# Strided attention of five batches on GpSimd and VectorE instead of TensorE, and TensorE's insertions regrouped

## The chip, the cores and the metric

The kernel runs on one core of a Trainium2 chip. TensorE multiplies matrices, VectorE and ScalarE work element by element from SBUF and PSUM, GpSimd from SBUF alone, and SyncE issues the transfers. The time is that of the device for one execution, in microseconds (us); the runs are summed up by their median.

## The reference, cut to what matters

Attention with 8 batches, 8 heads, 576 positions and 64 columns per head, then a mixer. Heads 0 to 3 see the last 32 positions, heads 4 to 7 see earlier positions with the same remainder by 32:

```python
rel = pos[:, None] - pos[None, :]
mask_local = (rel >= 0) & (rel < stride)
mask_strided = (rel >= 0) & (pos[None, :] % stride == pos[:, None] % stride)
attn = np.exp(scores - max); attn = attn / (sum + 1e-09); out = np.matmul(attn, v)
# x: the heads side by side, 8 x 576 x 512
h = np.maximum(xt @ w_tok1, 0.0) @ w_tok2      # xt: x transposed, 512 x 576; w_tok1 576 x 256
u = x + h.transpose(0, 2, 1)
out = u + np.maximum(u @ w_ch1, 0.0) @ w_ch2   # w_ch1 512 x 1536
```

A strided head is thus 32 separate causal attentions over 18 positions.

## The kernel before, in words

All matmuls of the mixer keep f32 precision by splitting each operand into a high and a low part (`xh` and `xlo`, `hh` and `hl`, `uh` and `ul`, `gh` and `gl`), and take three products. The 4608 tokens go through the channel mixer (`mlp`) in nine groups of 512. A group has 12 hidden tiles `fc`. `up_proj(fc)` is 12 matmuls into a PSUM tile `h` (two banks); ScalarE makes `gh` of it (L454), VectorE the residual `gl` (L455); `down_proj(fc)` is 12 matmuls into four accumulators `acc`, issued after `up_proj(fc + 2)`. At the end VectorE (L483) and GpSimd (L485) make `ot`, in two buffers, and SyncE stores it.

A group has 48 slots, four per tile, at which other work is put into TensorE's queue; that queue's order is as written. In group g the other work is for batch b = g + 1:

- attention in units. A strided unit (`strided_unit`) is two heads and half of the positions, four per batch; it packs three of the 18-position attentions into one 64 x 64 product (12 small matmuls for the scores, 3 transposes, 12 matmuls for the values). A local unit is two heads and 384 positions (24 + 3 + 24). Score tables are masked and their maximum taken by VectorE (L144), exponentiated by ScalarE (L147), the output scaled by VectorE (L191, L252). A strided unit loads `eq`, `ek`, `ev`, a local one `lq`, `lk`, `lv`; both store to DRAM (`xs`, `xl`). Group 0 has four units, group 1 eight, groups 2 to 5 seven, group 6 six.
- at slot 33 or later `do_load` brings `x` of the batch back from DRAM with rows of one position in one partition; five slots later `tok1` multiplies it by `w_tok1` in five chunks, for each of which ScalarE makes `xh` (L292) and VectorE `xlo` (L293), two buffers each; then `tok2` transposes `x` into the same PSUM tile as the second product and makes `uh`, `ul` for the next group (its rest at slots 2 and 4 of that group).

A unit is a generator that is sent PSUM tiles in three steps. Before, one insertion holds the values of unit k - 2, the transposes of unit k - 1 and the scores of unit k, and shares one pair of banks:

```python
pair = [ps_t.tile() for _ in range(2)]
if av: av.send([t[:, :DT] for t in pair])
if tr: tr.send(ps_h.tile("h"))
if qk: qk.send([t[:, DT:] for t in pair])
```

The order on the other engines, SyncE's transfers included, is made by a scheduler from priorities and modelled times when the kernel is built; at run time each engine takes its queue in that fixed order and waits where an operand is missing.

Of the kernel before, what the change touches and what calls it, by code (L numbers as in the profile page):

```python
# [19 lines left out]
HL = 4  # L20
# [46 lines left out]
@with_exitstack  # L67
def attn_mixer_kernel(ctx, tc, qT, kT, vw, qsT, ksT, vsP, mask, w1, w2, wt1, wt2, outT):
    nc = tc.nc
# [437 lines left out]

    pools = {n: ctx.enter_context(tc.tile_pool(name=n, bufs=2, reuse_waits="tile")) for n in ("sp", "wk")}
    NS = 4 * NFC
    local_order = [(p, hp, c0) for p in range(1, B // 2) for c0 in (0, 3, 6) for hp in range(2)]  # L510

    for g in range(NG):
# [15 lines left out]

# [4 lines left out]
        if b < B:  # L533
            units = [lambda hp=hp, half=half: strided_unit(pools["sp"], pools["wk"], ps_t, b, hp, half) for hp in range(2) for half in range(2)]
            if g:
                n = 4 if g == 1 else 3
                for _ in range(n):
                    if local_order:
                        p, hp, c0 = local_order.pop(0)
                        units.append(lambda p=p, hp=hp, c0=c0: local_unit(pools["late"], pools["wk"], ps_t, p, hp, c0, 3))  # L540
                order = [u for pair in zip(units[:4], units[4:]) for u in pair] + units[4 + min(4, len(units) - 4):]
                order += [u for u in units if u not in order]
                units = order
# [5 lines left out]
            live = [None] * len(units) + [None] * 2  # L549

            def load(k, u, live=live):
                live[k] = u()
                next(live[k])

            def go(k, live=live):
                insert(live[k - 2] if k > 1 else None, live[k - 1] if 0 < k <= len(live) - 2 else None, live[k] if k < len(live) - 2 else None)

            for k, u in enumerate(units):
                at(max(0, first + tick * k - 6), lambda k=k, u=u: load(k, u))
            for k in range(len(units) + 2):  # L560
                at(first + tick * k, lambda k=k: go(k))
            last = first + tick * (len(units) + 1)
# [14 lines left out]
def _layout(q, k, v, moe_w_tok1, moe_w_tok2, moe_w_ch1, moe_w_ch2):  # L577
# [42 lines left out]
    for m in range(3):  # L620
        for a in range(4):
# [23 lines left out]
```

## Time and profile before

| | |
|---|---|
| median of 3 runs | 930.91 us (928.67 to 931.06) |
| the profiled execution | 929.39 us |
| its span (first to last instruction) | 927.6 us |
| TensorE / VectorE / ScalarE / GpSimd busy | 875.5 / 329.0 / 309.6 / 82.4 us |
| a group with seven units (group 5) | 97 us |
| a group without units (group 7) | 75 us |

All durations below come from the profiled execution. A group is counted from the end of the one before; its first microseconds hold the rest of the last one's output. "Busy" on TensorE is modelled per matmul; the distance between starts tells the pace.

### The profile page before, as it was taken

How to read it: one execution, taken by the hardware profiler on the slowest of the kernel's cores; microseconds unless marked ns; L12 is line 12 of the kernel's file. 1: busy time of each engine (PE TensorE's matmuls, PEld its weight loads, DVE VectorE, ACT ScalarE, POOL GpSimd, SP SyncE). 2: the span in 40 equal slices, each digit the busy share in tenths (PEclk: the TensorE clock that was granted, in tenths of full speed). 3: DMA queues.
4: the chain of work that ended last, by engine and by line, in shares of the span. 5: the costliest groups of instructions: out<-in, count | busy, mean ns of one | idle time of the engine just before them, and what ended most of it. 6: DMA issues, size and time to landing. Idle time of an engine off the chain costs nothing.

```text
span 927.6 us, 18575 instructions
## 1 busy us (share of the span) xinstructions
PE 875.5 (94%) x7412; PEld 694.8 (75%) x7412; DVE 329.0 (35%) x1215; ACT 309.6 (33%) x1085; POOL 82.4 (9%) x68
## 2 busy tenths in 40 slices
PE   5677899999989999999999999999999999999996
PEld 3455677787768877887778777877788787788885
DVE  4977772333323232323223333333233323111212
ACT  6755352225422343225322542145214421110110
POOL 1324330010001000020002000200020002001100
PEclk9998799999999999999999999999999999999999
DMA  8665752113440144014411351124311211000001
GB/s 276 200 206 165 222 169 64 42 46 100 119 134 23 56 117 143 16 61 122 128 44 46 109 157 43 46 71 142 97 46 33 74 42 46 1 1 24 23 1 46
DMA packets 65431, 81.21 MB, mean 88 GB/s; under 512 B 6976, under 2 KB 53440, under 8 KB 65344
## 3 DMA queue, kind: packets, MB, share of 16 engines
q1 hardware_dynamic: 65344, 80.01, 28.8%
q8 instruction: 59, 0.97, 0.4%
q14 instruction: 28, 0.23, 0.1%
HBM read 61.57 MB, written 18.28 MB: 86 GB/s over the span
## 4 chain that ended last, share of the span: by engine, by line
PE 83%; DMA 6%; DVE 5%; ACT 2%; SPq 2%; issue 1%; DVEq 0%; POOL 0%; ACTq 0%; POOLq 0%
PE acc L465 31%; PE h L451 30%; PE t L61 20%; PE h L64 2%; DMA w_raw<-in_w 1%; DVE w_f L103 1%; DVE w_f L104 1%; DMA xs<-ax 1%; DMA out_t<-ot 1%; DVE xlo L293 1%; SPq L275 1%; ACT as L147 1%; ACT xh L292 1%; DMA ev<-in_vsP 1%; DMA w_raw<-in_wt 1%
## 5 line engine op out<-in xcount | busy, mean ns | idle before, releaser
L451 PE MATMUL h<-uh,w1h 128*128 128x512 f32 x432 | 173.5, 402 | 5.1 <-DVE gl L455 5.1
L465 PE MATMUL acc<-gh,w2h 128*128 128x512 f32 x432 | 172.9, 400 | 0.0
L451 PE MATMUL h<-ul,w1h 128*128 128x512 f32 x432 | 170.5, 395 | 0.0
L451 PE MATMUL h<-uh,w1l 128*128 128x512 f32 x432 | 169.6, 393 | 0.0
L465 PE MATMUL acc<-gl,w2h 128*128 128x512 f32 x432 | 169.0, 391 | 0.0
L465 PE MATMUL acc<-gh,w2l 128*128 128x512 f32 x432 | 168.6, 390 | 0.0
L455 DVE SCALAR_TENSOR_TENSOR gl<-h,gh 128x512 fp32r<-128x512 f32 x108 | 74.5, 690 | 234.4 <-ACT gh L454 234.2
L454 ACT ACTIVATE gh<-h 128x512 fp32r<-128x512 f32 x108 | 64.1, 594 | 253.2 <-PE h L451 253.0
L147 ACT ACTIVATE as<-as,am 128x64 f32<-128x64 f32 x336 | 112.5, 336 | 44.8 <-DVE am L144 44.8
L485 POOL TENSOR_TENSOR ot<-ot,ul 128x512 f32<-128x512 f32 x32 | 40.6, 1290 | 687.5 <-DVE ot L483 687.5
L451 PEld LDWEIGHTS h<-uh,w1h 128*128 128x128 f32 x432 | 81.9, 190 | 23.5 <-DVE gl L455 5.6
L451 PEld LDWEIGHTS h<-uh,w1l 128*128 128x128 f32 x432 | 82.0, 190 | 17.3
L465 PEld LDWEIGHTS acc<-gh,w2l 128*128 128x128 f32 x432 | 81.3, 188 | 17.7
L465 PEld LDWEIGHTS acc<-gh,w2h 128*128 128x128 f32 x432 | 81.3, 188 | 17.7
L451 PEld LDWEIGHTS h<-ul,w1h 128*128 128x128 f32 x432 | 82.0, 190 | 16.1 <-DVE ul L349 0.3
L465 PEld LDWEIGHTS acc<-gl,w2h 128*128 128x128 f32 x432 | 81.3, 188 | 15.4
L144 DVE CUSTOM_DVE_ANT_0 as<-t,mask_sb 128x64 f32<-128x64 f32 x336 | 53.0, 220 | 36.0 <-PE t L61 29.5
L349 DVE TENSOR_TENSOR ul<-t,uh 128x512 fp32r<-128x512 f32 (+7 forms) x64 | 29.2, 457 | 100.0 <-ACT uh L348 99.9
L147 ACT ACTIVATION_READ_ACCUMULATOR as<-as,am 128x1 f32 x336 | 63.0, 187 | 0.0
L348 ACT CAST uh<-t 128x512 fp32r<-128x512 f32 (+7 forms) x64 | 25.3, 399 | 109.4 <-PE t L61 109.0
L293 DVE TENSOR_TENSOR xlo<-x,xh 128x512 fp32r<-128x512 f32 (+1 forms) x45 | 29.7, 678 | 56.0 <-ACT xh L292 56.0
L292 ACT CAST xh<-x 128x512 fp32r<-128x512 f32 (+1 forms) x45 | 24.8, 571 | 59.2 <-PE t L61 24.9
(62 smaller groups left out, 938.3 us busy)
## 6 DMA issues: line engine op xcount, KB each, us to landing
w_raw<-in_w SPq DMA_DIRECT2D x24, 512.0 KB
out_t<-ot SPq DMA_DIRECT2D x36, 256.0 KB
lv<-in_vw SPq DMA_DIRECT2D x20, 384.0 KB
ev<-in_vsP SPq DMA_DIRECT2D x32, 192.0 KB
eq<-in_qsT SPq DMA_DIRECT2D x32, 167.0 KB
ek<-in_ksT SPq DMA_DIRECT2D x32, 167.0 KB
lk<-in_kT SPq DMA_DIRECT2D x20, 208.0 KB
x<-xs SPq DMA_DIRECT2D x32, 128.0 KB
```

The lines of the kernel that those rows point to most:

```text
L61: self.tc.stamp_issue_order_token(self.tc.nc.tensor.matmul(*args, **how).ins, self.pool.name)
L144: nc.vector.tensor_tensor_reduce(out=s_t[:, c, j, :], in0=sc[j][:, 64 * c:64 * c + 64], in1=mask_sb[:, m, :], scale=-SCALE, scalar=TOP, op ...
L147: nc.scalar.activation(out=s_t[:, c, j, :], in_=s_t[:, c, j, :], func=AF.Exp, bias=m_t[:, c, j:j + 1], scale=-1.0, accum_out=z_t[:, c, j:j ...
L292: nc.scalar.copy(out=xh, in_=x)
L293: nc.vector.tensor_tensor(out=xlo, in0=x, in1=xh.bitcast(F32), op=ALU.subtract)
L348: nc.scalar.copy(out=uh, in_=pu)
L349: nc.vector.tensor_tensor(out=ul, in0=pu, in1=uh.bitcast(F32), op=ALU.subtract)
L451: nc.tensor.matmul(ph, l[:, cc, fs], r, start=(cc == 0 and k == 0), stop=(cc == NCC - 1 and k == 2))
L454: nc.scalar.activation(out=gh, in_=ph, func=AF.Relu)
L455: nc.vector.scalar_tensor_tensor(out=gl, in0=ph, scalar=0.0, in1=gh.bitcast(F32), op0=ALU.max, op1=ALU.subtract)
L465: nc.tensor.matmul(acc[cc], l[:, fc, cs], r, start=(fc == 0 and k == 0), stop=(fc == NFC - 1 and k == 2))
L485: add.tensor_tensor(out=o_t, in0=o_t, in1=ul.bitcast(F32), op=ALU.add)
```

## The change

Batches 0 to 2 (`NPE = 3`) keep their strided units. For batches 3 to 7 a new function `strided(pool, b)` puts one attention of 18 positions of one head into each of the 128 partitions (4 heads x 32). For query i GpSimd multiplies its 64 columns with those of each key up to i, at most nine keys an instruction, and VectorE sums over the columns; then softmax over a table of 18 x 18; then for each i GpSimd multiplies weights and values and VectorE sums over the keys. That is 27 products and 27 sums in either half, with two buffers `sprod` between the engines. The result goes to DRAM in the order of positions, so `load_x` fetches it in three transfers instead of eight. It is issued in group g for batch g + 2, with a priority behind everything else, into pool `sp` with one buffer, which opens late in group 1 where the strided units' pool `third` closes.

The insertions change too: the scores of unit k stand with the transposes of unit k - 1, and the values of a unit stand apart, each with a pair of banks of its own. Groups 2 to 6 keep only local units, one each six slots.

```diff
+def strided(pool, b):
+        q_t = pool.tile([P, NJ, D], F32, name="sa")
+        k_t = pool.tile([P, NJ, D], F32, name="sb")
+        nc.sync.dma_start(out=q_t, in_=qs[b - NPE])
+        nc.sync.dma_start(out=k_t, in_=ks[b - NPE])
...
+        for i in range(NJ):
+            for n0 in range(0, i + 1, NJ // 2):
+                n = min(i + 1 - n0, NJ // 2)
+                pr = pool.tile([P, NJ * D // 2], F32, name="sprod", bufs=2)[:, :n * D].rearrange("p (n d) -> p n d", d=D)
+                nc.gpsimd.tensor_tensor(out=pr, in0=k_t[:, n0:n0 + n], in1=q_t[:, i:i + 1].to_broadcast([P, n, D]), op=ALU.mult)
+                nc.vector.tensor_reduce(out=s_t[:, i, n0:n0 + n], in_=pr, axis=AX.X, op=ALU.add)
+        v_t = pool.tile([P, D, NJ], F32, name="sa")
+        nc.sync.dma_start(out=v_t, in_=vs[b - NPE])
...
+        o_t = pool.tile([P, NJ, D], F32, name="sb")
+        for i in range(NJ):
+            n = i + 1
+            nd = D if n <= NJ // 2 else D // 2
+            for d0 in range(0, D, nd):
+                pr = ...
+                nc.gpsimd.tensor_tensor(
+                    out=pr, in0=v_t[:, d0:d0 + nd, :n], in1=s_t[:, i:i + 1, :n].to_broadcast([P, nd, n]), op=ALU.mult)
+                nc.vector.tensor_reduce(out=o_t[:, i, d0:d0 + nd], in_=pr, axis=AX.X, op=ALU.add)
+        for h in range(HL):
+            nc.sync.dma_start(out=xd[1][b][:, D * h:D * h + D].rearrange("(j r) c -> r j c", r=ST), in_=o_t[ST * h:ST * h + ST])
...
-        def insert(av, tr, qk):
-            pair = [ps_t.tile() for _ in range(2)]
...
+        def scores(u, before):
+            if u:
+                u.send([ps_t.tile() for _ in range(2)])
+            if before:
+                before.send(ps_h.tile("h"))
...
-            first, tick = (6, 3) if g else (10, 5)
+            first, tick, half_tick, ahead = ((10, 5, 3, 6), (6, 3, 2, 4))[g] if g < 2 else (6, 6, 3, 4)
...
+                at(t, lambda k=k: qk(k))
+                at(t + tick + half_tick, lambda k=k: av(k))
...
+            if g == 1:
+                at(last + 1, third_ends)
+            if g and g + 2 < B:
+                at(i0, lambda: do_strided(g + 2))
```

How the instructions move on the engines is seen at four places. The lines are those of either kernel: after the change the numbers are higher (L293 `xlo` is L331, L455 `gl` is L493, L483 `ot` is L521).

TensorE, group 5, one insertion between large matmuls (`ev`, `ek`, `eq` of strided units, `as` the score table, `ident` the transposes), before:

```order
L451 MATMUL h<-uh,w1l 128x512
L61 MATMUL t<-ev,as 64x64 x12
L64 MATMUL h<-ident,as 128x128 x3
L61 MATMUL t<-ek,eq 64x64 x12
L451 MATMUL h<-uh,w1h 128x512
```

and after the change, group 3, where only local units (`lk`, `lq`) are left:

```order
L503 MATMUL acc_4476<-gh,w2l 128x512
L62 MATMUL t<-lk,lq 32x64 x24
L65 MATMUL h<-ident,as 128x128 x3
L503 MATMUL acc_4477<-gh,w2h 128x512
```

The values no longer stand there, and there are fewer such places.

VectorE, the token mixing of a middle group and what follows it, before (group 5):

```order
L455 SCALAR_TENSOR_TENSOR gl<-h,gh 128x512
L252 TENSOR_TENSOR ax<-t,az 128x3x64 x2
L455 SCALAR_TENSOR_TENSOR gl<-h,gh 128x512
L293 TENSOR_TENSOR xlo<-x,xh 128x512 x2
L455 SCALAR_TENSOR_TENSOR gl<-h,gh 128x512
L293 TENSOR_TENSOR xlo<-x,xh 128x512 x3
L305 SCALAR_TENSOR_TENSOR hl_7289<-t,hh_7288 128x512
L305 SCALAR_TENSOR_TENSOR hl_7291<-t,hh_7290 128x512
L349 TENSOR_TENSOR ul<-t,uh 128x128 x4
L483 TENSOR_TENSOR ot<-acc_6396,uh 128x512
L483 TENSOR_TENSOR ot<-acc_6397,uh 128x512
```

and after the change (group 3; `ss<-sprod` is a sum of products, `sm` the maximum of the strided softmax):

```order
L283 TENSOR_REDUCE ss<-sprod 128x7
L283 TENSOR_REDUCE ss<-sprod 128x9
L331 TENSOR_TENSOR xlo<-x,xh 128x512
L283 TENSOR_REDUCE ss<-sprod 128x8
L331 TENSOR_TENSOR xlo<-x,xh 128x512
L283 TENSOR_REDUCE ss<-sprod 128x9
L331 TENSOR_TENSOR xlo<-x,xh 128x512
L283 TENSOR_REDUCE ss<-sprod 128x9
L286 TENSOR_REDUCE sm<-ss 128x18
L287 TENSOR_TENSOR ss<-ss,sm 128x324
L343 SCALAR_TENSOR_TENSOR hl_5307<-t,hh_5306 128x512
L343 SCALAR_TENSOR_TENSOR hl_5309<-t,hh_5308 128x512
```

Between the `xlo` of chunks 2, 3 and 4 there stands a sum, which waits for a product of GpSimd.

VectorE a little later, at the border to group 4, after the change (`sb<-sprod` are sums of the value half):

```order
L387 TENSOR_TENSOR ul<-t,uh 128x256
L521 TENSOR_TENSOR ot<-acc_4475,uh 128x512
L521 TENSOR_TENSOR ot<-acc_4476,uh 128x512
L301 TENSOR_REDUCE sb<-sprod 128x64 x2
L493 SCALAR_TENSOR_TENSOR gl<-h,gh 128x512
L521 TENSOR_TENSOR ot<-acc_4477,uh 128x512
L301 TENSOR_REDUCE sb<-sprod 128x32 x2
L521 TENSOR_TENSOR ot<-acc_4478,uh 128x512
L493 SCALAR_TENSOR_TENSOR gl<-h,gh 128x512
```

Before, only `ot` stood ahead of the first `gl` there; now sums stand among them.

SyncE in the next group, after the change (`xs_87<-sb` is the strided result of batch 5, `x<-xs_87` its way back):

```order
L524 DMA out_t<-ot 128x512 x4
L158 DMA lq<-in_qT 128x384
L159 DMA lk<-in_kT 128x416
L272 DMA sa<-in_qs 128x1152
L303 DMA xs_87<-sb 32x18x64 x4
L158 DMA lq<-in_qT 128x384
L159 DMA lk<-in_kT 128x416
L317 DMA x<-xs_87 128x4x256
L319 DMA x<-xs_87 64x256 x2
L273 DMA sb<-in_ks 128x1152
L160 DMA lv<-in_vw 128x768
```

The store, which waits for the last sum of batch 5, stands ahead of a local unit's `lq` and `lk`; the load of the next batch's keys (`sb<-in_ks`) stands behind them.

## Rows read from the trace of the kernel before

**Rows 1.** The page: busy time of each engine with its share of the span and its instructions; then the chain of work that ended last, as shares by engine.

```profile
PE 875.5 (94%) x7412; PEld 694.8 (75%) x7412; DVE 329.0 (35%) x1215; ACT 309.6 (33%) x1085; POOL 82.4 (9%) x68
...
PE 83%; DMA 6%; DVE 5%; ACT 2%; SPq 2%; issue 1%; DVEq 0%; POOL 0%; ACTq 0%; POOLq 0%
```

**Rows 2.** The table of stretches, group 5 (with batch 6) and group 7 (no attention work beside it). Columns: the stretch in us, its length, busy us and instructions of TensorE, of its weight loads, of VectorE, ScalarE and GpSimd, TensorE's granted clock as a share of 2.4 GHz, the share of the DMA engines, GB/s.

```profile
590.00:687.00 97.00, 96.39 (x886) 76.93 (x885) 30.81 (x137) 33.21 (x125) 5.08 (x4) 1.00 0.29 84
...
783.00:858.00 75.00, 75.00 (x336) 61.06 (x335) 13.10 (x20) 9.52 (x16) 5.08 (x4) 1.00 0.04 15
```

**Rows 3.** VectorE's timeline, the residual `gl` of a hidden tile: of group 5 tile 3, tile 7 and tile 10, of group 6 tile 3, tile 4 and tile 10, of group 7 tile 3 and tile 10. Columns: start and length in us, engine, line, operation, out<-in, shapes, count, and in brackets the idle time before and what ended it.

```profile
606.65 0.69 DVE L455 SCALAR_TENSOR_TENSOR gl<-h,gh 128x512 fp32r<-128x512 f32 x1 [0.94 <-ACT gh L454]
...
636.69 0.69 DVE L455 SCALAR_TENSOR_TENSOR gl<-h,gh 128x512 fp32r<-128x512 f32 x1 [2.11 <-ACT gh L454]
...
659.79 0.69 DVE L455 SCALAR_TENSOR_TENSOR gl<-h,gh 128x512 fp32r<-128x512 f32 x1 [4.30 <-ACT gh L454]
...
704.54 0.69 DVE L455 SCALAR_TENSOR_TENSOR gl<-h,gh 128x512 fp32r<-128x512 f32 x1 [0.82 <-ACT gh L454]
...
710.66 0.69 DVE L455 SCALAR_TENSOR_TENSOR gl<-h,gh 128x512 fp32r<-128x512 f32 x1 [2.09 <-ACT gh L454]
...
755.42 0.69 DVE L455 SCALAR_TENSOR_TENSOR gl<-h,gh 128x512 fp32r<-128x512 f32 x1
...
802.51 0.69 DVE L455 SCALAR_TENSOR_TENSOR gl<-h,gh 128x512 fp32r<-128x512 f32 x1 [0.67 <-ACT gh L454]
...
840.53 0.69 DVE L455 SCALAR_TENSOR_TENSOR gl<-h,gh 128x512 fp32r<-128x512 f32 x1 [4.75 <-ACT gh L454]
```

**Rows 4.** TensorE's timeline around one insertion in group 5 (large matmul before, values of a local unit's neighbour, transposes, scores, large matmuls after), and the first scores of a later insertion. The profile counts each small f32 matmul twice.

```profile
629.52 0.39 PE L465 MATMUL acc<-gh,w2l 128*128 128x512 f32 x1
629.84 0.58 PE L61 MATMUL t<-ev,as 64*64 64x64 f32 x24
630.35 0.55 PE L64 MATMUL h<-ident,as 128*128 128x128 f32 x3
630.88 0.84 PE L61 MATMUL t<-ek,eq 64*64 64x64 f32 x24
631.65 0.50 PE L465 MATMUL acc<-gh,w2h 128*128 128x512 f32 x1
631.98 0.39 PE L465 MATMUL acc<-gl,w2h 128*128 128x512 f32 x1
...
637.71 0.52 PE L61 MATMUL t<-lk,lq 64*32 64x64 f32 x6 [0.54 <-DVE ax L191]
```

**Rows 5.** GpSimd: all instructions of the output's second addition (name, count, shortest/median/longest in ns, first and last start, shapes), the one instruction on 256 columns, and, from its timeline, the longest one.

```profile
L485 POOL TENSOR_TENSOR ot<-ot,ul x32: 1278/1290/1297, 183.9 to 859.8; 128x512 f32<-128x512 f32 x32
...
L126 POOL TENSOR_TENSOR t1l<-w_f,t1h x1: 727/727/727, 25.5 to 25.5; 64x256 fp32r<-64x256 f32 x1
...
111.44 1.74 POOL L116 TENSOR_TENSOR w1l<-w_f,w1h 128x512 fp32r<-128x512 f32 x1 [1.30 <-ACT w1h L115]
```

**Rows 6.** VectorE: the subtraction `xlo` in all its uses (shortest/median/longest in ns), the scaling of a strided unit's output (busy us, mean ns | idle us), and from the timeline two score tables that follow each other directly.

```profile
L293 DVE TENSOR_TENSOR xlo<-x,xh x45: 408/692/1501, 26.6 to 766.5; 128x512 fp32r<-128x512 f32 x35, 128x256 fp32r<-128x256 f32 x10
...
L252 DVE TENSOR_TENSOR ax<-t,az 128x192 f32<-128x192 f32 x64 | 19.9, 352 | 35.1 <-PE t L61 35.1
...
607.85 0.22 DVE L144 CUSTOM_DVE_ANT_0 as<-t,mask_sb 128x64 f32<-128x64 f32 x1 [0.51 <-PE t L61]
...
608.00 0.22 DVE L144 CUSTOM_DVE_ANT_0 as<-t,mask_sb 128x64 f32<-128x64 f32 x1
```

**Rows 7.** The timeline of ScalarE, VectorE and TensorE's weight loads in group 4's token mixing of batch 5: chunk 2's `xh` and `xlo` and the weight load that takes it; chunk 4's `xlo` and the weight load that takes it.

```profile
569.79 0.62 ACT L292 CAST xh<-x 128x512 fp32r<-128x512 f32 x1 [2.12 <-PE t L61]
570.45 0.69 DVE L293 TENSOR_TENSOR xlo<-x,xh 128x512 fp32r<-128x512 f32 x1 [2.05 <-ACT xh L292]
...
571.20 0.19 PEld L61 LDWEIGHTS t<-xlo,t1h 128*128 128x128 f32 x1 [0.28 <-DVE xlo L293]
...
573.31 0.69 DVE L293 TENSOR_TENSOR xlo<-x,xh 128x512 fp32r<-128x512 f32 x1 [0.81 <-ACT xh L292]
...
574.05 0.18 PEld L61 LDWEIGHTS t<-xlo,t1h 64*128 64x128 f32 x1 [0.50 <-DVE xlo L293]
```

**Rows 8.** The timeline near 30 us, in the part before the groups: two GpSimd subtractions that follow each other, a VectorE `xlo` on 256 columns beside them, and the matmul that waits for it.

```profile
30.22 3.07 POOL L116 TENSOR_TENSOR t2l<-w_f,t2h 128x512 fp32r<-128x512 f32 x2 [3.98 <-ACT t2h L115]
...
30.67 1.49 DVE L293 TENSOR_TENSOR xlo<-x,xh 128x256 fp32r<-128x256 f32 x1
...
32.21 0.58 PE L61 MATMUL t<-xlo,t1h 128*128 128x256 f32 x1 [1.07 <-DVE xlo L293]
```

**Rows 9.** The timeline at the border between groups 4 and 5: the third `ot` of group 4, `gl` of group 5's tile 0, and the first matmul of the third `up_proj`.

```profile
589.52 0.69 DVE L483 TENSOR_TENSOR ot<-acc,uh 128x512 f32<-128x512 f32 x1 [2.94 <-DMA out_t<-ot]
...
590.13 0.68 DVE L455 SCALAR_TENSOR_TENSOR gl<-h,gh 128x512 fp32r<-128x512 f32 x1
...
591.58 0.39 PE L451 MATMUL h<-uh,w1h 128*128 128x512 f32 x1
```

**Rows 10.** The chain of work that ended last: a load of `lq`, a store of attention output to DRAM, and SyncE issuing a transfer (start and length in us).

```profile
30.18 3.25 DMA lq<-in_qT
...
260.72 2.46 DMA xs<-ax
...
263.33 0.31 SPq L275
```

More of the change, by code (lines that the diff above doesn't have):

```diff
@@ L35 @@
 FIRST = {0: 1, 4: 2}
+NPE = 3
 NCC = DM // P
@@ L153, in local_unit @@
     def local_unit(pool, work, ps_t, p, hp, c0, n, into=None):
-        q_t = pool.tile([P, UC * P], F32, name="lq")[:, :n * P]
-        k_t = pool.tile([P, UC * P + 32], F32, name="lk")[:, :n * P + 32]
+        q_t = pool.tile([P, UC * P], F32, name="lq", bufs=1 if p else 2)[:, :n * P]
+        k_t = pool.tile([P, UC * P + 32], F32, name="lk", bufs=1 if p else 2)[:, :n * P + 32]
         v_t = pool.tile([P, 4 * UC, D], F32, name="lv")[:, :4 * n]
@@ L270, in load_x @@
         src = xd[half][b]
-        if half:
+        if half and b < NPE:
             src = src.rearrange("(r j) d -> r j d", j=NJ)
@@ L506, in staging_ends, with third_ends, do_strided @@
         pools["late"] = ctx.enter_context(tc.tile_pool(name="late", bufs=2, side="right", reuse_waits="tile"))
-    pools = {n: ctx.enter_context(tc.tile_pool(name=n, bufs=2, reuse_waits="tile")) for n in ("sp", "wk")}
+    pools = {"wk": ctx.enter_context(tc.tile_pool(name="wk", bufs=2, reuse_waits="tile"))}
+    third = tc.tile_pool(name="third", bufs=2, reuse_waits="tile")
+    pools["third"] = third.__enter__()
+    def third_ends():
+        third.__exit__(None, None, None)
+        pools["sp"] = ctx.enter_context(tc.tile_pool(name="sp", bufs=1, reuse_waits="tile"))
+    def do_strided(b):
+        now = tc.cur_priority
+        tc.cur_priority = now + 3000
+        strided(pools["sp"], b)
+        tc.cur_priority = now
     NS = 4 * NFC
@@ L533, in attn_mixer_kernel @@
         if b < B:
-            units = [lambda hp=hp, half=half: strided_unit(pools["sp"], pools["wk"], ps_t, b, hp, half) for hp in range(2) for half in range(2)]
+            st, loc = [], []
+            if b < NPE:
+                st = [lambda hp=hp, half=half: strided_unit(pools["third"], pools["wk"], ps_t, b, hp, half) for hp in range(2) for half in range(2)]
             if g:
[L536 to L543, printed above, removed]
+                for p, hp, c0 in local_order[:4 if g == 1 else 3]:
+                    loc.append(lambda p=p, hp=hp, c0=c0: local_unit(pools["late"], pools["wk"], ps_t, p, hp, c0, 3))
+                del local_order[:len(loc)]
+            units = [u for k in range(4) for us_ in (st, loc) for u in us_[k:k + 1]]
             if g == 0:
@@ L547, in attn_mixer_kernel @@
                 at(NS - 1, staging_ends)
-            first, tick = (6, 3) if g else (10, 5)
-            live = [None] * len(units) + [None] * 2
+            first, tick, half_tick, ahead = ((10, 5, 3, 6), (6, 3, 2, 4))[g] if g < 2 else (6, 6, 3, 4)
+            live = [None] * len(units)
             def load(k, u, live=live):
@@ L553, in load, with qk, av @@
                 next(live[k])
-            def go(k, live=live):
-                insert(live[k - 2] if k > 1 else None, live[k - 1] if 0 < k <= len(live) - 2 else None, live[k] if k < len(live) - 2 else None)
+            def qk(k, live=live):
+                scores(live[k] if k < len(live) else None, live[k - 1] if k else None)
+            def av(k, live=live):
+                live[k].send([ps_t.tile() for _ in range(2)])
             for k, u in enumerate(units):
[L559 to L562, printed above, removed]
+                t = first + tick * k
+                at(max(0, t - ahead), lambda k=k, u=u: load(k, u))
+                at(t, lambda k=k: qk(k))
+                at(t + tick + half_tick, lambda k=k: av(k))
+            at(first + tick * len(units), lambda: qk(len(live)))
+            last = first + tick * len(units) + half_tick
             i0 = max(last + 2, 33)
@@ L608, in grp_t @@
         return np.concatenate([a, np.zeros((B, HL // 2, P, TW * NT + TC - TW - S), a.dtype)], axis=3)
+    qs, ks = (c(grp(a)[NPE:]).reshape(B - NPE, P, NJ, D) for a in (q, k))
+    vs = c(grp(v)[NPE:].transpose(0, 1, 2, 4, 3)).reshape(B - NPE, P, D, NJ)
     vsP = np.zeros((B, HL, NT * TW, D), v.dtype)
```

22 lines of the change are left out of this document (14 added, 8 removed).

## The prediction

> **What bounds the kernel now.** I read the page first: TensorE is busy 94% of the span and makes 83% of the chain that ended last [rows 1]. A busy TensorE is no proof of a full one, so the second view is the table of stretches: from 590 to 687 us (group 5 with batch 6 beside it) TensorE shows 96.4 of 97 us at a granted clock of 1.00 (2.4 GHz), VectorE 31, GpSimd 5 [rows 2]. The third is the cadence inside it. The residual `gl` comes once per hidden tile, and where nothing is inserted (group 7) seven tiles take 840.53 - 802.51 = 38.0 us, 168 large matmuls at 0.226 us each. In group 5 the same seven take 659.79 - 606.65 = 53.1 us, with four strided and three local units between, and in group 6 755.42 - 704.54 = 50.9 us, with four and two [rows 3]. The reader is to see that in groups 2 to 6 the attention's small matmuls sit on the path one for one: what leaves TensorE's queue shortens the group, and what TensorE waits for lengthens it.
>
> **TensorE's gain.** A local unit costs 53.14 - 50.88 = 2.3 us (rounded) in such a stretch, so four strided units cost 53.1 - 38.0 - 3 x 2.3 = 8.3 us. One insertion seen singly agrees: from the last matmul before it (629.52) to the second after it (631.98) stand 2.46 us, of which two cadences are 0.45, so 2.0 us for a unit's values, transposes and scores [rows 4]. Its edges cost 0.1 us each: 629.52 to 629.84 and 631.65 to 631.98 instead of 0.23. The change splits what stood in one place into two, so in groups 2 to 5 three units now need seven places (four more than the three that the 2.3 us cover), 4 x 0.2 = 0.8 us. Gain 8.3 - 0.8 = 7.5 us, and 7.7 in group 6 with two units: 4 x 7.5 + 7.7 = **-37.7 us**. In groups 0 and 1 all units stay, and the places grow from 6 to 9 and from 10 to 17: 10 x 0.2 = **+2 us**; 0 if the smaller pieces pack as before, 7 if each new place also waits for a bank as one does now (0.54 us) [rows 4].
>
> **The work that moves.** Per batch GpSimd makes 2 x 171 x 64 = 21,888 products per partition in 54 instructions, and VectorE sums them in 54. No row shows GpSimd with a repeated operand; the nearest are 1.29 us for 512 elements, 0.73 for 256 [rows 5], so 2.2 ns an element and 0.17 us an instruction: 47.7 + 9.2 = 57 us per batch. From below, all at the 2.5 ns that `ot` has without any fixed part, 55; from above, the 1.74 us that one 512 took beside two-input VectorE work [rows 5], 3.4 ns an element: 74. I take 57: `ot` reads and writes whole tiles with VectorE at work beside it and stays within 1.28 to 1.30. A sum is shown nowhere either; a VectorE subtraction takes 0.69 for 512 and 0.41 for 256 [rows 6], 1.11 ns and 0.12 us: 24 + 7 = 31 us, 24 with nothing fixed. The four units that leave took 4 x (6 x 0.15 + 2 x 0.35) = 6.4 us and four reciprocals from VectorE, near 7 [rows 6]. So VectorE rises from 31 to about 57 of 89 us (2 of it softmax) and GpSimd from 5 to 62: neither is full. Both are hidden under TensorE as long as the order lets them be, and that order is where the gain can be lost. ScalarE and SyncE only lose work.
>
> **Where the order bites.** VectorE is a queue, and each sum in it waits for its product, with two product buffers. Behind a late product stand `gl`, `xlo`, `ul` and the score tables. `gl` of a tile is wanted by `down_proj` two tiles on, so in mid-group it has some 8 us. Three places have none.
>
> First, the token mixing. In the stretch at 570 us `xh` of chunk 2 ends at 570.41, `xlo` at 571.14 and TensorE takes it at 571.20; for chunk 4 `xlo` ends at 574.00 and is taken at 574.05 [rows 7]. Three chunks per batch hang on VectorE with at most 0.2 us to spare. Behind the change a sum stands between each two of these `xlo`, and GpSimd multiplies meanwhile. At 30.67 `xlo` on 256 columns took 1.49 us beside GpSimd's 1.5 us instructions, against 0.41 [rows 6, 8], and TensorE waited 1.07 us for it. So the two hinder each other. If every `xlo` met GpSimd half way through a product of 576 elements (0.17 + 576 x 2.2 ns = 1.4 us) it would lose 0.7 us; I take 0.65, since TensorE has a little to spare: 3 x 0.65 x 5 groups = **+9.8 us**. Bounds: 0 if the buffers are full and GpSimd idles there; whole product and sum ahead each time, 1.4 + 0.8 = 2.2 us, 15 times: 33.
>
> The Trainium skill, "SBUF — State Buffer", section "Who interferes with whom", says that a VectorE instruction with two SBUF inputs and a GpSimd instruction that reads SBUF exclude each other for the whole of an instruction, and that `tensor_reduce` never does. By that the sums run free, each `xlo` can lose up to one product, 15 x 1.4 = 21 us at most, and the trace agrees as far as it shows pairs [rows 8].
>
> Second, the group's border. `gl` of tile 0 ends at 590.81 and the third `up_proj`, which needs the bank that it empties, begins at 591.58: 0.8 us to spare, and already now the third `ot` waits 2.9 us for an output transfer [rows 9]. Now sums stand ahead of `gl`, and GpSimd's part of `ot`, which frees that transfer, stands between products. One late product of 1.4 us less the 0.8: 0.6, and a little for `ot`: 0.8 x 5 = **+4 us** (0 to 14, two products late).
>
> Third, SyncE. In each of groups 2 to 6 the store of the strided result stands ahead of a later unit's `lq` and `lk`. From the last sum, a store's issue is 0.3 us; transfers take 2.5 to 3.3 us to land [rows 10]. The window for a batch, from `gl` 7 of a group to `gl` 4 of the next, is 710.66 - 636.69 = 74.0 us [rows 3] less some 4 for units that go and 3 for the load: 67. GpSimd's need is 57 plus some 5 in which softmax lets it idle: 62. It fits by 5 us: **+2 us** for odd lateness (0 to 15).
>
> Sum, against the profiled execution of 929.39 us (span 927.6): 929.4 - 37.7 + 2 + 9.8 + 4 + 2 = 909.5. The median of the runs is 930.91, 1.5 above that execution, so **911.0 us**.
>
> **Rivals.** *Nothing is given back*: VectorE and GpSimd run ahead of TensorE, all three waits are nought. For it: both have a third of each group free. Against: `xlo` has no slack. 929.4 - 37.7 + 2 = 893.7, so 895 us. *The token mixing eats the gain*: every `xlo` loses a whole product and a sum, 33 us instead of 9.8: 932.7, so 934 us, slower than before. It decides from (37.7 - 2 - 6) / 15 = 2.0 us per `xlo`; the longest seen is 1.1 over its price [rows 6, 8], which speaks against it. *GpSimd is the bound*: products at 3.4 ns make 74 + 5 = 79 us against the window of 67, so 12 us late in each of five batches through SyncE and `gl`: 60 in place of the 2 and 9.8 and 4: 953.7, so 955 us. It cancels the gain from (37.7 - 2) / 5 = 7 us over the window, 74 us per batch or about 2.75 ns an element. For it: the price with a repeated or strided operand isn't in the trace. *The change doesn't do what it says*: excluded by the instruction order, in which the units are gone.
>
> **How the numbers follow.** Forecast (part given back, 897 to 927) 0.68; nothing given back 0.12; token mixing 0.11; GpSimd 0.09. The range 894 to 932 leaves out GpSimd as the bound, half of the token mixing's case, and the odd run below 894. About 0.3% (2.8 us) is what a measurement of this kernel tells from no change, so the same lies from 928.1 to 933.7. Faster: 0.68 + 0.12 + a part of the token mixing's case that stops short, 0.05 = 0.85; same 0.05; slower 0.10.
>
> **What would show it.** Right: in a middle group seven tiles take near 46 us instead of 53.1; GpSimd about 57 us busy per batch, products of 576 at 1.4 us, sums of 576 near 0.76; TensorE's new waits in the token mixing on `xlo`, some 2 us a group, and under 1 us at `gl` 0. Wrong: products over 1.6 us; waits for `lq` of several us in each group; `gl` of mid-group on the list of TensorE's waits; or no wait on `xlo` at all. What would make it wrong most easily is a GpSimd price that no row here shows.

## The result, and the profile after

The changed kernel takes **898.14 us** (median of 4 runs, 896.59 to 900.71) against 930.39 us for the kernel before beside it: ratio 0.966, 95% interval 0.963 to 0.969. Forecast were 911.0 us and a range of 894 to 932. The sign and the range held; the sum was 13 us too long, and its terms were further off than that, in opposite directions.

The page of the kernel after: busy time of each engine, share of the span and instructions; then the chain that ended last, which answers to [rows 1].

```profile
PE 835.1 (93%) x6392; PEld 665.7 (74%) x6392; DVE 449.3 (50%) x1215; ACT 255.4 (29%) x810; POOL 361.8 (40%) x343
...
PE 56%; POOL 12%; DMA 12%; DVE 10%; SPq 4%; ACT 4%; issue 2%; DVEq 0%; ACTq 0%; POOLq 0%
```

TensorE has lost 40 us of work and still is the bound, but now shares the chain with GpSimd and VectorE. In the table of stretches (columns as in [rows 2]) each row is one group, from the first of its first 24 `up_proj` matmuls to that of the next group; groups 2 to 6.

```profile
289.40:383.10 93.70, 89.25 (x682) 71.95 (x681) 60.90 (x148) 23.14 (x71) 64.22 (x64) 0.98 0.30 90
383.10:477.10 94.00, 88.83 (x682) 71.95 (x681) 57.62 (x142) 22.43 (x70) 66.69 (x65) 0.96 0.28 83
477.10:570.00 92.90, 89.78 (x683) 71.97 (x682) 57.73 (x144) 22.56 (x70) 66.83 (x67) 0.98 0.28 84
570.00:661.20 91.20, 88.84 (x682) 71.56 (x681) 57.74 (x142) 22.57 (x70) 66.71 (x65) 1.00 0.29 86
661.20:748.10 86.90, 86.83 (x583) 70.77 (x582) 27.38 (x70) 19.50 (x55) 13.79 (x12) 1.00 0.14 44
```

The reader is to compare the length with TensorE's busy time: 2 to 5 us of each group but the last are idle, the granted clock over a whole group falls to 0.96, and group 6, which has no GpSimd work at its end, loses nothing. In group 5 the seven tiles of [rows 3] run from `gl` 3 to `gl` 10 in 47.8 us instead of 53.1:

```profile
589.58 0.69 DVE L493 SCALAR_TENSOR_TENSOR gl<-h,gh 128x512 fp32r<-128x512 f32 x1 [0.30 <-ACT gh L492]
...
637.41 0.68 DVE L493 SCALAR_TENSOR_TENSOR gl<-h,gh 128x512 fp32r<-128x512 f32 x1
```

The prices of the moved work, from the list of costliest groups (busy us, mean ns | idle before):

```profile
L282 POOL TENSOR_TENSOR sprod<-sb,sa 128x576 f32<-128x576 f32 (+6 forms) x135 | 141.1, 1075 | 150.1 <-DMA sb<-in_ks 128.8 <-DVE ss L283 21.0
L299 POOL TENSOR_TENSOR sprod<-sa,ss 128x448 f32<-128x448 f32 (+7 forms) x135 | 136.9, 1046 | 29.1 <-DVE ss L292 21.6 <-DVE sb L301 7.0
L301 DVE TENSOR_REDUCE sb<-sprod 128x64 f32<-128x64 f32 (+8 forms) x135 | 76.3, 570 | 29.5 <-POOL sprod L299 28.5
L283 DVE TENSOR_REDUCE ss<-sprod 128x9 f32<-128x576 f32 (+6 forms) x135 | 75.2, 571 | 67.3 <-POOL sprod L282 66.6
```

That is (141.1 + 136.9) / 5 = 55.6 us of products and (75.2 + 76.3) / 5 = 30.3 us of sums per batch. GpSimd waits for VectorE's sums only 28 us in all.

What TensorE waits for in groups 2 to 5 together (waited for: us in total, times, longest):

```profile
PE t L62 <- DVE xlo L331: 12.1, 5, 5.2
PE h L489 <- DVE gl L493: 2.3, 2, 2.2
```

The longest of these waits is the only one of group 3. VectorE, ScalarE and TensorE around it (start, length, what ended the idle time before), and the table of stretches from its end on:

```profile
452.68 0.62 ACT L330 CAST xh<-x 128x512 fp32r<-128x512 f32 x1 [1.91 <-PE t L62]
...
453.80 0.55 DVE L283 TENSOR_REDUCE ss<-sprod 128x6 f32<-128x384 f32 x1 [0.22 <-POOL sprod L282]
455.17 0.75 DVE L283 TENSOR_REDUCE ss<-sprod 128x9 f32<-128x576 f32 x1 [0.81 <-POOL sprod L282]
455.84 0.68 DVE L493 SCALAR_TENSOR_TENSOR gl<-h,gh 128x512 fp32r<-128x512 f32 x1
456.43 0.61 DVE L283 TENSOR_REDUCE ss<-sprod 128x7 f32<-128x448 f32 x1
457.61 0.75 DVE L283 TENSOR_REDUCE ss<-sprod 128x9 f32<-128x576 f32 x1 [0.57 <-POOL sprod L282]
458.28 1.07 DVE L331 TENSOR_TENSOR xlo<-x,xh 128x512 fp32r<-128x512 f32 x1
...
453.85 0.39 PE L62 MATMUL t<-xh,t1h 128*128 128x512 f32 x1
459.40 0.79 PE L62 MATMUL t<-xlo,t1h 128*128 128x512 f32 x1 [5.17 <-DVE xlo L331]
460.00 0.63 PE L62 MATMUL t<-xh,t1l 128*128 128x512 f32 x1
460.42 0.63 PE L62 MATMUL t<-xh,t1h 128*128 128x512 f32 x1
...
459.40:463.00 3.60, 3.60 (x9) 2.82 (x10) 2.83 (x4) 0.62 (x1) 3.04 (x2) 0.50 0.00 0
```

`xh` is ready at 453.30. `xlo` starts at 458.28 since VectorE's fixed queue has four sums and a `gl` ahead of it: 1.6 us of that time (0.22 + 0.81 + 0.57) VectorE is idle for products, the rest it is at work on what stands ahead. Then `xlo` takes 1.07 us instead of 0.69. Of TensorE's 5.2 us nearly all is the standing in order; it is 3.8 us in group 2 and 1.5 in group 5, so some 10 of the 12.1 us. And the wait leaves something behind: matmuls that came every 0.227 us now come every 0.43, up to 463, at a granted clock of 0.50 (the 1.2 GHz level instead of 2.4).

### The profile page after: what moved, and what is told of

Read it like the earlier page. It is cut to its first block, busy times and chain, and to the rows that moved or that the text cites. A ratio compares the mean times of both kernels' runs of the same rounds, so it can differ in the third digit from the quotient of the medians.

```text
span 894.8 us, 16269 instructions
## 1 busy us (share of the span) xinstructions
PE 835.1 (93%) x6392; PEld 665.7 (74%) x6392; DVE 449.3 (50%) x1215; ACT 255.4 (29%) x810; POOL 361.8 (40%) x343
## 4 chain that ended last, share of the span: by engine, by line
PE 56%; POOL 12%; DMA 12%; DVE 10%; SPq 4%; ACT 4%; issue 2%; DVEq 0%; ACTq 0%; POOLq 0%
PE h L489 21%; PE acc L503 21%; PE t L62 14%; POOL sprod L282 7%; POOL sprod L299 4%; DVE xlo L331 2%; DMA x<-xl 2%; DVE w_f L104 2%; DMA xs<-sb 1%; DVE ss L283 1%; DMA sb<-in_ks 1%; DVE w_f L105 1%; DMA w_raw<-in_w 1%; SPq L217 1%; DMA xs<-ax 1%
## 5 line engine op out<-in xcount | busy, mean ns | idle before, releaser
L282 POOL TENSOR_TENSOR sprod<-sb,sa 128x576 f32<-128x576 f32 (+6 forms) x135 | 141.1, 1075 | 150.1 <-DMA sb<-in_ks 128.8
L493 DVE SCALAR_TENSOR_TENSOR gl<-h,gh 128x512 fp32r<-128x512 f32 x108 | 74.1, 687 | 166.4 <-ACT gh L492 166.1
L299 POOL TENSOR_TENSOR sprod<-sa,ss 128x448 f32<-128x448 f32 (+7 forms) x135 | 136.9, 1046 | 29.1 <-DVE ss L292 21.6
L523 POOL TENSOR_TENSOR ot<-ot,ul 128x512 f32<-128x512 f32 x32 | 41.3, 1302 | 201.0 <-DVE ot L521 200.8
L283 DVE TENSOR_REDUCE ss<-sprod 128x9 f32<-128x576 f32 (+6 forms) x135 | 75.2, 571 | 67.3 <-POOL sprod L282 66.6
L503 PEld LDWEIGHTS acc<-gh,w2l 128*128 128x128 f32 x432 | 81.2, 188 | 17.5
L489 PEld LDWEIGHTS h<-ul,w1h 128*128 128x128 f32 x432 | 82.0, 190 | 15.7
L148 ACT ACTIVATE as<-as,am 128x64 f32<-128x64 f32 x216 | 72.5, 338 | 69.6 <-DVE am L145 69.6
L301 DVE TENSOR_REDUCE sb<-sprod 128x64 f32<-128x64 f32 (+8 forms) x135 | 76.3, 570 | 29.5 <-POOL sprod L299 28.5
L62 PE MATMUL t<-xlo,t1h 128*128 128x512 f32 (+3 forms) x90 | 41.0, 456 | 17.1 <-DVE xlo L331 16.8
```

What stands on the lines that cost most here:

```text
L62: self.tc.stamp_issue_order_token(self.tc.nc.tensor.matmul(*args, **how).ins, self.pool.name)
L148: nc.scalar.activation(out=s_t[:, c, j, :], in_=s_t[:, c, j, :], func=AF.Exp, bias=m_t[:, c, j:j + 1], scale=-1.0, accum_out=z_t[:, c, j:j ...
L282: nc.gpsimd.tensor_tensor(out=pr, in0=k_t[:, n0:n0 + n], in1=q_t[:, i:i + 1].to_broadcast([P, n, D]), op=ALU.mult)
L283: nc.vector.tensor_reduce(out=s_t[:, i, n0:n0 + n], in_=pr, axis=AX.X, op=ALU.add)
L299: nc.gpsimd.tensor_tensor(out=pr, in0=v_t[:, d0:d0 + nd, :n], in1=s_t[:, i:i + 1, :n].to_broadcast([P, nd, n]), op=ALU.mult)
L301: nc.vector.tensor_reduce(out=o_t[:, i, d0:d0 + nd], in_=pr, axis=AX.X, op=ALU.add)
```

## The experiments

Group lengths tell more than totals. Each is counted from the first of the 24 consecutive `up_proj` matmuls at a group's head to the next group's; groups 0 and 1 stand together because half of a `tok2` lies in one or the other. Group 7 has 73.8 us in every kernel.

| kernel | median us | ratio to before beside it (95%) | groups 0 + 1 | groups 2 to 6 |
|---|---|---|---|---|
| before | 930.39 | 1 | 234.7 | 481.6 |
| changed | 898.14 | 0.966 (0.963 to 0.969) | 225.7 | 458.7 |
| regrouping alone | 906.53 | 0.977 (0.975 to 0.979) | 221.3 | 472.4 |
| offload alone | 907.63 | 0.978 (0.974 to 0.982) | 229.9 | 464.2 |
| no strided work | 870.87 | 0.937 (0.935 to 0.939) | 220.8 | 437.1 |
| before, further inputs | 928.73 | 1.000 (0.998 to 1.001) | 232.2 | 481.9 |
| before, pools swapped | 921.88 | 0.992 (0.990 to 0.994) | 227.1 | 481.9 |
| before, scores ahead | 936.39 | 1.007 (1.005 to 1.009) | 235.7 | 487.8 |
| batch after the last `xlo` | 880.61 | 0.947 (0.945 to 0.949) | 225.2 | 445.0 |
| that, one place | 896.86 | 0.964 (0.961 to 0.967) | 231.9 | 452.3 |
| that, keys loaded before | 883.95 | 0.951 (0.949 to 0.954) | 225.3 | 445.1 |

**Regrouping alone.** The changed kernel with `NPE = 8`, so the old load of `x` and no `do_strided`; the changed order of the SBUF pools stays in it:

```diff
-NPE = 3
+NPE = 8
-            first, tick, half_tick, ahead = (...)[g] if g < 2 else (6, 6, 3, 4)
+            first, tick, half_tick, ahead = (...)[g] if g < 2 else (6, 3, 2, 4)
```

> All strided units stay on TensorE, two buffers for lq and lk, no new inputs; only the grouping of the insertions is that of the changed kernel. Theory of the prediction (a split insertion costs 0.2 us): 10 more places in groups 0 and 1 and about 6 more in each of groups 2 to 6, +2 and +6 us, so 936 to 940 us, group 0 (first gl of group 0 to first gl of group 1) at 103.6 us as before. Rival 'regrouping gains': the 9 us that the changed kernel gained in group 0, the start and group 7 come from the grouping; then group 0 is near 96 us and the whole at 918 to 924.

Measured 906.5 us, 23 us faster, so both expectations were wrong. Some 8 of the 23 belong to the pools' order (measured alone below: 921.9 us), so the grouping is worth some 15: the part that I had priced at a loss carries as much as the offload. The gain is in every group, 1.7 to 1.9 us in each of groups 2 to 6. TensorE's timeline has the reason: values alone, then scores with the transposes behind them.

```profile
501.10 0.39 PE L466 MATMUL acc<-gh,w2l 128*128 128x512 f32 x1
501.42 0.58 PE L62 MATMUL t<-ev,as 64*64 64x64 f32 x24
501.93 0.50 PE L452 MATMUL h<-uh,w1h 128*128 128x512 f32 x1
502.26 0.39 PE L452 MATMUL h<-ul,w1h 128*128 128x512 f32 x1
...
503.19 0.40 PE L452 MATMUL h<-uh,w1l 128*128 128x512 f32 x1
503.52 0.58 PE L62 MATMUL t<-ek,eq 64*64 64x64 f32 x24
504.03 0.55 PE L65 MATMUL h<-ident,as 128*128 128x128 f32 x3
504.33 0.48 PE L452 MATMUL h<-uh,w1h 128*128 128x512 f32 x1
504.64 0.39 PE L452 MATMUL h<-ul,w1h 128*128 128x512 f32 x1
```

Two places take 1.16 + 1.45 us, less two cadences of 0.45 each 1.71; the one place of [rows 4] took 2.46 - 0.45 = 2.01. So a unit is 0.30 us cheaper in two places, although the second place does cost its 0.2; for seven units that is 2.1 us, near what a group gains. What got shorter is the start of the next instruction behind the transposes (0.53 to 0.30 us) and behind the scores (0.77 to 0.51).

**Scores ahead of the transposes, in the kernel before.** To see whether the order made that gain:

```diff
-            if tr:
-                tr.send(ps_h.tile("h"))
             if qk:
                 qk.send([t[:, DT:] for t in pair])
+            if tr:
+                tr.send(ps_h.tile("h"))
```

> The kernel before with one line moved: at each insertion the scores of the next unit go ahead of the transposes of the unit before, so values, scores, transposes instead of values, transposes, scores; still one place. If the regrouping's gain is the border from transposes to scores (0.53 us behind the transposes instead of 0.30, and 0.77 to 0.90 behind the scores instead of 0.51 to 0.65), each unit is 0.45 to 0.5 us shorter, 7 units in groups 2 to 6 give 3.1 to 3.5 us a group (93.0 to 93.4 us), groups 0 and 1 give 5 to 6, and the whole is 907 to 909 us. Rival: the gain comes from taking the values apart; then 929 to 931 us.

Measured 936.4 us, slower than before: the order is not it. A stretch of TensorE there, with VectorE's scaling of the values beside it:

```profile
523.64 0.58 PE L61 MATMUL t<-ev,as 64*64 64x64 f32 x24
524.69 0.83 PE L61 MATMUL t<-ek,eq 64*64 64x64 f32 x24 [0.46 <-DVE ax L252]
525.45 0.55 PE L64 MATMUL h<-ident,as 128*128 128x128 f32 x3
525.75 0.48 PE L451 MATMUL h<-uh,w1h 128*128 128x512 f32 x1
...
524.27 0.62 DVE L252 TENSOR_TENSOR ax<-t,az 128x192 f32<-128x192 f32 x2 [1.70 <-PE t L61]
```

The scores wait for `ax`, VectorE's reading of the values, because `insert` puts values and scores into two halves of one PSUM tile. There are two tiles, one per head, and two `ax`; the first scores start 0.06 us after the first `ax` ends and the second head's only after the second, which is why the scores stay long (0.76). In the kernel before, the transposes covered part of that wait, and here nothing does. The kernel before shows the same by itself. Below are the first scores of its group 2, which have no values ahead of them in their place and the next matmul 0.51 us behind them; and, for the insertion of [rows 4], whose next matmul comes 0.77 us behind the scores, the weight loads of these:

```profile
316.00 0.58 PE L61 MATMUL t<-ek,eq 64*64 64x64 f32 x24
316.51 0.50 PE L465 MATMUL acc<-gh,w2h 128*128 128x512 f32 x1
...
630.88 0.70 PEld L61 LDWEIGHTS t<-ek,eq 64*64 64x64 f32 x24 [0.22 <-DVE ax L252]
```

So the regrouping gains because scores get PSUM tiles of their own and no longer stand behind VectorE: 0.23 + 0.26 us, less 0.2 for the further place. The Trainium skill, "PSUM — Partial Sum Buffer", section "PSUM bank collisions raise a hardware error", asks for a semaphore between engines on one PSUM bank, by bank and quadrant. The trace agrees in that scores wait for VectorE's reading of the other half of their tile, 0.46 us here. One place with four tiles wasn't tried.

**Offload alone.** The changed kernel with the `insert` of before (values, transposes, scores in one place; ticks (10, 5), (6, 3) and then (6, 6)).

> The strided heads of batches 3 to 7 go to GpSimd and VectorE as in the changed kernel, but the insertions keep the grouping of the kernel before (values of one unit, transposes of the next, scores of the one after in one place, sharing two PSUM tiles), in groups 0 and 1 with its ticks, in groups 2 to 6 every six slots. If the offload carries the whole gain and the grouping is worth its 0.2 us a place, 896 to 900 us with group 0 at 96 us; if group 0's gain belongs to the grouping, group 0 is at 103 us and the whole at 904 to 908.

Measured 907.6 us, where the second theory put it, but group 0 is short as the first had it (97.0 us from its first `gl` to the next group's, 103.7 before), so neither holds; groups 0 and 1 are 4.9 us shorter than before. 22 us alone and 23 for the regrouping, but 32 together: both kernels have the new pools, whose 8 us are counted twice in the sum, and the two overlap in the units that leave, which can't be made cheaper as well.

**Where groups 0 and 1 got shorter.** Two kernels ask for the cause. One declares `qs`, `ks`, `vs` in the kernel before and never reads them:

> The kernel before with the three further inputs declared and nothing else changed (they are never read). If the place of the inputs in memory, or what comes with them, made group 0 shorter, group 0 is near 96 us and the whole at 920 to 924; if it belongs to the grouping or to the pools, group 0 stays at 103.6 and the whole within 0.3% of 930.4.

It measured 928.7 us: not the inputs. The other swaps two names:

```diff
-    pools = {n: ... for n in ("sp", "wk")}
+    pools = {n: ... for n in ("wk", "sp")}
```

> The kernel before with its two pools sp and wk made in the other order, so that the strided units' tiles and the scores' tiles stand at other places of SBUF; no instruction is added or left out. If group 0 is shorter in the changed kernel because its tiles take over other places, the first TensorE matmul of group 2 is near 293 us (298.2 before) and the whole near 925 us; if the pools are no part of it, 930 us.

It measured 921.9 us, -8 us from the order in which two SBUF pools are made. SyncE's queue before (start, length, what is issued), what SyncE waits for there from 88 to 93 us, and its queue with the pools swapped:

```profile
88.23 0.38 SPq L207 DMA_DIRECT2D xl<-ax  x1
91.94 0.33 SPq L226 DMA_DIRECT2D eq<-in_qsT  x1
...
94.75 0.84 SPq L98 DMA_DIRECT2D w_raw<-in_w  x2
```

```profile
SPq L226 <- DMA xl<-ax: 3.3, 1, 3.3
```

```profile
86.80 0.38 SPq L207 DMA_DIRECT2D xl<-ax  x1
87.23 0.47 SPq L226 DMA_DIRECT2D eq<-in_qsT  x1
...
90.26 13.07 SPq L98 DMA_DIRECT2D w_raw<-in_w  x5
```

Before, the load of `eq` waited 3.3 us for the store of an attention output `ax`, and the weight loads behind it in SyncE's queue with it. I take it that the tile `eq` lay where that `ax` had been; the trace shows the wait and not the addresses. Group 0 shortens by 8.3 us: TensorE's waits for `ul` in it fall from 4.3 to 0.4 us, and its granted clock over the group is 0.96 instead of 0.90. The diff makes `wk` first and has the same order of starts (87.04, 87.47, 90.45). The pool's move is part of the diff, and no step of the prediction priced it.

**No strided work.** `x`'s strided half of batches 3 to 7 is filled from `xd[0]`, and `do_strided` is not called.

> Leaves out the strided heads of batches 3 to 7 altogether (their half of x is filled with the local heads); everything else as in the changed kernel. Its distance to the changed kernel is all that GpSimd's and VectorE's work costs TensorE. Theory 'the waits and the clock after them are the price': 12.8 us of waits for xlo, 2.3 for gl and the clock of 0.96 to 0.98 in groups 1 to 4 go, 878 to 884 us, with xlo at 0.69 us each. The prediction's rival of nothing given back put this case at 895; if the time is 893 or more, the waits of the changed kernel were hidden and its price is near 5 us.

Measured 870.9 us, 7 us below the lowest expectation. It splits the offload: against the regrouping alone the 20 units cost TensorE 35.8 us (groups 0 to 6: 693.7 to 657.9, 1.8 us a unit), and GpSimd's and VectorE's work gives back 684.4 - 657.9 = **26.5 us** of it. Of those, some 18.5 are TensorE's added waits (group 1 `xh` 3.4, groups 2 to 5 4.5, 5.2, 3.1, 2.4). The other 8 are mostly matmuls at the lower clock behind them: in groups 1 to 4 TensorE is at work for 16.3 us at a granted clock of 0.50, and for 3.4 us without strided work, which at half the pace is 6.4 us lost. In group 3 it is 94.0 - 87.0 - 5.2 = 1.8; without strided work this group runs wholly at 1.00:

```profile
372.20:459.20 87.00, 86.96 (x683) 70.55 (x682) 24.06 (x76) 22.28 (x69) 5.20 (x5) 1.00 0.21 63
```

**Sums alone, products alone.** To part VectorE's standing from GpSimd's reading, one half is left out each time.

Of each kernel's edit one line stands here:

```diff
-                nc.gpsimd.tensor_tensor(out=pr, ...)      # sums alone: pr is one fixed tile
-                nc.vector.tensor_reduce(out=..., in_=pr)  # products alone: nobody reads pr, the output is set to zero
```

> Leaves out GpSimd's products of batches 3 to 7: VectorE forms the same sums, from one fixed tile that is filled once a batch, so nothing makes them wait and GpSimd reads nothing beside them. With the sums' 30 us a batch alone on VectorE. Theory 'VectorE stands in order behind sums whose products come late' and theory 'GpSimd's reads stretch the subtractions' both say 870 to 876 us (no strided work at all gave 870.9), no wait for xlo over 1 us and xlo at 0.69 us. If it is VectorE's plain load that costs, the time stays at 885 us or more.

Measured 931.2 us, against every expectation. With nothing to pace them, the sums of several batches ran in groups 1 and 2 (124.9 and 123.9 us; VectorE busy 111.6 us of group 2), where TensorE waited for `xlo`, `ul`, `gl` and `ax`; groups 3 to 6 were as short as without strided work. As a test of the changed kernel it is void. It shows one thing: near 405 us an `xh` is ready at 404.78, its `xlo` takes 0.68 us and yet starts at 409.70, behind sums that wait for nothing. TensorE waits up to 4.7 us for an `xlo` there: standing in order costs by itself.

> Leaves out VectorE's sums of batches 3 to 7: GpSimd forms the same products, which nobody reads, the scores stay masked and the output of these heads is zero. 'Standing in order' says 870 to 874 us: no sum stands ahead of xlo any more, even if an xlo meets a product and takes 1.1 to 1.6 us. 'Stretched by GpSimd's reads' says 5 groups with at least 3 xlo each 0.4 to 0.9 us longer and TensorE waiting for them as in the changed kernel, 880 us or more.

Its runs lay between 895 and 920 us, so the time decides nothing. There is a trace of the longest of them, and none of the others. `xlo` (shortest/median/longest ns), and VectorE's and GpSimd's timelines in group 1:

```profile
L330 DVE TENSOR_TENSOR xlo<-x,xh x45: 406/692/16132, 26.9 to 758.2; 128x512 fp32r<-128x512 f32 x35, 128x256 fp32r<-128x256 f32 x10
```

```profile
267.26 16.73 DVE L330 TENSOR_TENSOR xlo<-x,xh 128x512 fp32r<-128x512 f32 x2 [6.35 <-ACT xh L329]
...
261.90 20.95 POOL L282 TENSOR_TENSOR sprod<-sb,sa 128x576 f32<-128x576 f32 x19
282.90 1.06 POOL L293 MEMSET sb<- 128x1152 f32 x1
```

One subtraction of 512 elements took 16.1 us. It ended at 283.39, half a microsecond after GpSimd's last product (282.85), while GpSimd was already writing a memset. The same kernel once more:

> The kernel with GpSimd's products and without VectorE's sums once more (it leaves out the sums of batches 3 to 7), for a second trace: the first, of an execution of 919.99 us, showed xlo of 9.6 to 16.1 us. If unbroken products hold a subtraction with two SBUF operands out for their whole length, this trace too shows some xlo of several us, each ending within 1 us of the end of a row of products, and no gl above 0.70; if that belonged to the one execution, all xlo stay under 1.6 us.

919.6 us, and the same picture: four `xlo` of 15.8, 10.9, 10.2 and 14.3 us (in the first trace 16.1, 10.2, 9.6 and 14.3), the first ending at 280.47 with the last product at 279.92. All eight end 0.55 us after the last product of their row. How often this comes in the shorter runs is not shown. `gl`, whose other operand is in PSUM, stays below 0.70 us among the same products:

```profile
L492 DVE SCALAR_TENSOR_TENSOR gl<-h,gh x108: 673/691/693, 90.0 to 902.6; 128x512 fp32r<-128x512 f32 x108
```

The Trainium skill, "SBUF — State Buffer", section "Who interferes with whom", says that a VectorE instruction with two SBUF inputs and a GpSimd instruction that reads SBUF lock each other out for a whole instruction. The traces agree on who is hit (sums and `gl` keep their price) and go beyond it on how long: not one product, but the whole unbroken row, here up to 14. In the changed kernel GpSimd has to pause for VectorE's sums, and the longest `xlo` is 1.56 us.

**The batch begun after the last `xlo`.** GpSimd's batches in the changed kernel drift against the groups: the first product comes 71, 52, 48, 41 and 35 us after the head of groups 1 to 5, and the token mixing stands near 68 to 78, so the score sums meet it. A small product of the last `xlo`, written where the key tile is loaded, holds the batch back:

```diff
+        nc.gpsimd.tensor_tensor(out=k_t[:, 0], in0=state["xlo"][:, :D]..., in1=state["xlo"][:, :D]..., op=ALU.mult)
-                at(i0, lambda: do_strided(g + 2))
+                at(i1, lambda: do_strided(g + 2))
```

> The changed kernel with the strided batch begun only after the last xlo of the group's token mixing (a first small product of that xlo with itself into the key tile, 0.3 us, which the key load then overwrites). All sums then lie behind the five xlo. If the price lies at the token mixing, its waits of 18.6 us and the clock behind them go, 874 to 882 us, and no wait for xlo above 1 us. Rival: the sums then stand ahead of ul and gl at the group border, which TensorE waits for instead, 888 to 898 us with gl and ul waits of 3 us or more a group.

Measured **880.6 us**, faster than both kernels, 17.5 below the changed one. Groups 2 to 6 take 87.7, 89.5, 87.7, 93.2 and 86.9 us, 7.9 over the kernel without strided work instead of 21.6; no `xlo` of 512 elements exceeds 0.72 us, and in these groups TensorE waits for no `gl` and no `ul`:

```profile
375.90:465.40 89.50, 87.64 (x683) 70.46 (x682) 53.60 (x136) 22.78 (x70) 59.27 (x59) 1.00 0.29 87
```

Nearly the same work of GpSimd and VectorE as in the changed kernel's group 3 (59.3 against 66.7 us, 53.6 against 57.6), at a clock of 1.00. So more than half of the give-back, 14.2 of 26.5 us over groups 0 to 6, hung on when the batch met the token mixing and not on how much work it is. 12.3 us stay: 4.4 in groups 0 and 1, 2.5 and 5.1 in groups 3 and 5, where TensorE waits for `xh`, whose `x` waits for the strided store.

Two further kernels tried to better it. The first joins values, scores and transposes in one place again:

> The changed kernel with the strided batch begun after the last xlo, and the insertions in one place again in the order values, scores, transposes. Against that kernel with the values apart (880.6 us) 3 places less in each of groups 2 to 6 and 10 less in groups 0 and 1 at 0.18 us, so 4 to 5 us less, 875 to 877 us. Rival: scores, values and transposes in one place wait for a PSUM tile or for VectorE where the split places did not, 881 us or more.

896.9 us, the rival: the shared tile again (TensorE waits 11.4 us for `ax`, instead of 4.5, and 15.7 for `xh`, instead of 10.4). The second loads the keys before and holds only the sums back:

> As the kernel whose strided batch begins after the last xlo (880.6 us), but the small product of xlo goes into the score table instead of the key tile, so the keys are loaded before and only the sums wait for it (two products can run ahead, into the two buffers). The batch then begins some 4 us earlier (the key load's 3.9 us are out of its way) and its result is stored earlier; where the x load waited for that store (groups 3 and 5, 2.5 and 5 us over the kernel without strided work) it no longer does: 873 to 877 us. Rival: the two products that run ahead meet xlo, or the store was not what x waited for: 879 us or more.

884.0 us, the rival too, with groups 2 to 6 as long as in the other (445.1 and 445.0). In group 5 the batch did end some 2 us earlier, but the store stands behind the load of `x`'s first half in SyncE's queue, so it didn't go out earlier; TensorE still waits 2.7 us for `xh` there. What would free it is left open.

## Why the prediction was right or wrong

- **The bound and the prices** were right: TensorE's queue sets the pace; GpSimd 55.6 us a batch (57 forecast), VectorE 30.3 (31), products of 576 at 1.45 and 1.39 in the two halves (1.4), sums of 576 at 0.75 (0.76). By its own 2.2 ns an element the 47.7 us of products should read 48.2, which leaves the 57.
- **TensorE's gain** was mis-sized: -37.7 forecast for groups 2 to 6; without strided work they are 44.5 us shorter. The step that failed is "2.0 us for a unit's values, transposes and scores": 0.49 us of it was a wait for `ax`, and so the split was priced as a loss of 0.2 a place where it gains 0.3 a unit. The row that told it was on show: the last of [rows 4] has scores that waited 0.54 us for `ax`. I used it as the price of a bank in the upper bound and didn't ask which insertions have that wait already.
- **Groups 0 and 1** were forecast at +2 us; without strided work they are 13.9 shorter. 13.4 of it the kernel with the regrouping alone has too: 7.7 go with the pools' order, measured by itself, and the other 5.7 I put down to the regrouping. The regrouping is the same error; the pools' order stands in the diff and got no term.
- **The token mixing** was the right place. Forecast 9.8; TensorE's waits for `xlo` in groups 2 to 5 are 12.1 us. But the near agreement is luck: I took mutual hindering as the price, and group 3 shows standing in order: 5.0 us behind sums and 0.4 of stretching. I priced the one sum between two `xlo`; what cost was the row of four sums and a `gl` ahead of chunk 2's. The bound "whole product and sum ahead" was nearer, for one or two `xlo` per group rather than three.
- **What follows a wait** was left out: some 8 us, 6.4 of them matmuls at half the pace. So was group 1, where `xh` comes late (3.4 us).
- **The border and SyncE**: 4 and 2 forecast; `gl` cost 2.3 us in groups 4 and 5, and no wait for `lq` or `lk` was added.

By these, the give-back was forecast at 15.8 us and is 26.5; what the rest gains was -35.7 and is -58.4 over groups 0 to 6. The errors cancelled in part. The rival "nothing given back" named 895 us, 3 from the result, although 26 us were given back: a number that fits does not show its mechanism.

## What to carry to other kernels

Before pricing an insertion as work, ask of each piece what it waits for: a half of a PSUM tile that VectorE still reads, or an SBUF place that a store still empties, makes a wait that moves with the grouping or with the order of pools. Work that fills an idle engine needs a fixed phase: 56 us of products and 30 of sums beside TensorE cost 26 us when free-running and 12 when they began behind the token mixing. Measure the parts apart, and know what each run shares with the others: two changes of 22 and 23 us made 32, since a third, of 8, was in both.

## What the runs showed of the hardware

- Unbroken GpSimd products from SBUF held a VectorE subtraction with two SBUF operands out for 9.6 to 16.1 us (0.69 alone), 8 to 14 products long, eight times in two traces, each time until 0.55 us after the row's last product; with pauses for VectorE's sums between products the longest was 1.56. `gl` with an operand in PSUM, and sums of 576 elements with one operand, kept 0.69 and 0.75 us.
- After one wait of 5.2 us TensorE's matmuls came every 0.43 us instead of 0.227 for 3.6 us more, at a granted clock of 0.50; the clock over this group of 94 us was 0.96.
- GpSimd's product with a repeated operand costs what its addition of whole tiles does: a mean of 1075 and 1046 ns over a mean of some 405 elements, beside 1302 ns for the addition of 512.
